# The first loads of an attention and experts kernel: half a weight slice first, six units on GpSimd's queue, scores ahead for one unit only

## The chip, the cores and the metric

The kernel runs on one core of a Trainium2 chip. The metric is the device time of one execution in microseconds (us), lower is better: the median of three runs is 1036.33 us. The engines are called by what they do: TensorE multiplies matrices, VectorE and ScalarE work on elements, GpSimd is used for some element work and issues transfers, and SyncE only issues transfers. In the profile they stand as PE (with its weight loads as PEld), DVE, ACT, POOL and SP.

## What is computed

Three parts run one behind the other, cut here to what matters:

```python
# 1: decaying linear attention; 4 batches, 8 heads, 768 steps, 64 wide
gamma = 1.0 - 2.0 ** (-5.0 - np.arange(H))
for t in range(S):
    state = gamma[None, :, None, None] * state + einsum('bhd,bhe->bhde', k[:, :, t], v[:, :, t])
    y[:, :, t] = scale * einsum('bhd,bhde->bhe', q[:, :, t], state)
# 2: x is y as (3072, 512); two weights of 512 x 2048 and 2048 x 512
h = x @ w_in
x = where(h > 0, h, exp(minimum(h, 0)) - 1) @ w_out
# 3: experts; 8 of them, each takes its 384 best of the 3072 tokens
logits = x @ w_gate
out[mask_e] = maximum(x[mask_e] @ w1[e], 0) @ w2[e]
```

## The kernel before

**Attention.** The 768 steps are cut into 6 chunks of 128. A unit is one chunk of one batch, all 8 heads of it, so there are 24 units, numbered from 0 here; two units make a block of 256 tokens, and there are 12 blocks. Units 0 to 3 are the first chunks of the four batches. For a unit, `load_units` (L349) brings q and k in transposed form into the tile `qk` and k and v in plain form into `kv`, 512 KB each; both tags have two buffers, so unit k takes the buffers of unit k - 2. `scores` (L393) multiplies k by q into `sc`, `masks` (L409) multiplies by the decay mask into `A` (in the first chunks by `hmask`, later by a triangle out of `csb`, with q decayed beforehand), `attend` (L419) multiplies v by `A` into `py`, together with the state `st` in later chunks. `y_out` (L438) splits `py` into a rounded part `yH` on ScalarE and a rest `yL` on VectorE. `carry` (L451) makes the new state from k and the decayed v through `pu`, and counts the unit as done. `decays` (L370) multiplies v by its decay on VectorE, in place; in the first chunks that waits until `attend` has read v. The thread `attention` (L474) goes through the units in that order. Its flag `ahead` puts the scores of unit k + 1 before the attend of unit k, for k below 3 where that unit's loads are issued already.

**Weights of part 2.** `w_in` and `w_out` arrive as 64-bit floats, each in 8 slices of two halves. A half is a tile `rw` of 512 KB. `load_weights` (L499) issues them on SyncE's queue in the order of the list `slices`: w1 slice 0, w1 slice 1, w2 slice 0, w1 slice 2, w2 slice 1 and so on. Every half is narrowed by hand: `scales` (L526) scales the high words on ScalarE or VectorE, `narrow` (L540) makes one shift (TENSOR_SCALAR) and two merges (SCALAR_TENSOR_TENSOR) into `n_rw` on VectorE, `highs` (L571) rounds to `w1H` or `w2H` on ScalarE, `lows` (L583) subtracts into `w1L` or `w2L` on VectorE. Slice 0 is narrowed half by half, the others by pairs. 

**Products.** For block n and slice i, `first_product` (L598) needs `yH` and `yL` of both units of the block and slice i of w1; its 24 matmuls fill one of two banks `ph`. `elus` (L634) makes `e`, `gH` and `gL` of it on ScalarE and VectorE, with two buffers of each. `second_product` (L664) needs these and slice i of w2, 12 matmuls into `px`. `seconds` (L687) runs the second products in the order in which the first ones were issued. Blocks 0 and 1 are worked on together, slice by slice, as the weights come.

**Who sets the order.** Nothing is ordered at run time: each engine and each queue runs a fixed list in order, and waits where an operand is not there. The lists come from a scheduler that runs at build time. Every activity above is a thread with a rank (lower goes first), `Sched.run` always advances the thread whose next instruction can start first by the model in `Plan` (L95), and `Plan.note` (L162) books durations, buffers and transfers. Transfers are one queue in that model, with 310 bytes per ns, and 150 for a plain load of GpSimd. In the kernel before, `load_units` (rank 0) and `load_weights` (rank 1) share SyncE's queue. It issues, at the start: the two halves of unit 0's `qk` (256 KB each), `hmask` (512 KB), unit 0's `kv`, `csb` (326 KB), `rcs` (4.5 KB), unit 1's `qk` and `kv`, and then the weights, with the later units' loads in between.

The lines that issue these loads are short:

```python
yield on("SP", ap.slot("kv"), when=lambda: did["unit"] > k - 2)
...
ahead = k < 3 and did["unit_load"] > k + 1
if ahead:
    yield from scores(k + 1)
yield from attend(k)
```

Parts 1 and 2 overlap until about 650 us; then come the routing of the tokens and the experts, whose code is not touched. The accumulating transfers that GpSimd issues in part 3 (`w1L<-e1R`) have the size of a unit's `qk`, 512 KB.

Of the kernel before, what the change touches and what calls it, by code (L numbers as in the profile page):

```python
# [44 lines left out]
BUSY = 8  # L45
# [49 lines left out]
class Plan:  # L95
# [66 lines left out]
    def note(self, eng, op, out, ins):  # L162
        o = out.tensor.name
        start = max([self.free[eng]] + [self.ready.get(x.tensor.name, 0.0) + self.gap(x.tensor.name, eng) for x in ins])
        if eng != "PE" or self.writer.get(o) != "PE":
            start = max(start, self.used.get(o, 0.0) + 140)
        if eng == "PE":
            end = start + self.pe_cost(op, ins, start)
            if start > self.free[eng] + 20:
                end += 100  # L170
        else:
            end = start + self.cost(eng, op, out, ins)
        self.free[eng] = end
        self.writer[o] = eng
        if "dma" in op:
            nb = self.size(out if out.space != "DRAM" else ins[0]) * P * 4
            self.dma = max(self.dma, end + 600) + nb / (150.0 if op == "dma_start" and eng == "POOL" else 310.0)
            end = self.dma + 1300
        for x in ins:
            k = x.tensor.name  # L180
            self.used[k] = max(self.used.get(k, 0.0), end)
        self.used[o] = max(self.used.get(o, 0.0), end)
        self.ready[o] = max(self.ready.get(o, 0.0), end) if "dma" in op or eng == "PE" else end
# [107 lines left out]
def on(eng, *needs, when=None, rank=None):  # L291
    return eng, needs, when, rank
# [3 lines left out]
def body(ctx: ExitStack, tc, qkv, w_in, w_out, w_gate_t, w1, w2, hm, cst, rc, rmat, out, dbg=None):  # L296
# [3 lines left out]
    PE, ACT, DVE, POOL, SP = (  # L300
        Engine(e, n, plan)
        for e, n in ((nc.tensor, "PE"), (nc.scalar, "ACT"), (nc.vector, "DVE"), (nc.gpsimd, "POOL"), (nc.sync, "SP"))
    )
    engines = {"ACT": ACT, "DVE": DVE, "POOL": POOL}
    ctx.enter_context(tc.manual_schedule())
    sched = Sched(plan)
    did = Counter()
# [7 lines left out]
    rcs = cp.tile([P, 1 + E], F32, name="rcs")  # L315
# [17 lines left out]
    ap = Tiles(s1.enter_context(tc.tile_pool(name="ap", bufs=2)), plan, 2)  # L333
    csb = c1.tile([P, cst.shape[1]], F32, name="csb")
# [13 lines left out]

    def load_units():  # L349
        for k, (b, c) in enumerate(seq):  # L350
            yield on("SP", ap.slot("kv"), when=lambda: did["unit"] > k - 2)
            qk, kv = (ap.tile([P, 2, H * D], F32, tag=tag, name=f"{tag}{k}") for tag in ("qk", "kv"))
            for part in ([0], [1]) if k == 0 else ([0, 1],):
                SP.dma_start(qk[:, part[0] : part[-1] + 1], qkv[b, c][:, part[0] : part[-1] + 1])
            if k == 0:
                SP.dma_start(hmask, hm)
            SP.dma_start(kv, qkv[b, c][:, 2:])
            if k == 0:
                SP.dma_start(csb, cst)
                SP.dma_start(rcs, rc)  # L360
            units[k] = {
                "qT": qk[:, 0].rearrange("p (a b) -> p a b", a=NP),
                "kT": qk[:, 1].rearrange("p (a b) -> p a b", a=NP),
                "k": kv[:, 0].rearrange("p (h d) -> p h d", h=H),
                "v": kv[:, 1].rearrange("p (h d) -> p h d", h=H),
                "q0": qk[:, 0],
            }
            did["unit_load"] += 1
# [24 lines left out]
    def scores(k):  # L393
        if k < 4:
            spare["tags"] = ("at", "at", "am", "m")
        elif k < 2 * tail + 2 and did["xcopy"] > 1:
            spare["tags"] = ("at", "at", "am")
        else:
            spare["tags"] = ("at", "at")
        yield on("PE", bank_slot(spare_tag()), *([csb] if seq[k][1] else []), when=lambda: did["decay_q" if seq[k][1] else "unit_load"] > k)  # L400
        u = units[k]
        u["sc"] = [spare_bank(f"sc{k}_{hh}") for hh in range(2)]
        for pr in range(NP):
            for hh in range(2):
                yield on("PE", u["q0"])
                sl = slice(hh * D, hh * D + D)
                PE.matmul(u["sc"][hh][:, pr * P : (pr + 1) * P], u["kT"][sl, pr, :], u["qT"][sl, pr, :], start=True, stop=True)

    def masks(k):  # L409
        u = units[k]  # L410
        u["A"] = []
        for hh in range(2):
            mask = tri if seq[k][1] else hmask[:, hh * NP * P : (hh + 1) * NP * P].rearrange("p (a b) -> p a b", a=NP)
            yield on("DVE", u["sc"][hh], ap.slot(f"A{hh}", 1), mask)
            a = ap.tile([P, NP, P], F32, tag=f"A{hh}", bufs=1, name=f"A{k}_{hh}")
            DVE.tensor_tensor(a, u["sc"][hh].rearrange("p (a b) -> p a b", a=NP), mask, op=OP.mult)
            u["A"].append(a)

    def attend(k):  # L419
        b, c = seq[k]  # L420
        yield on("PE", bank_slot(spare_tag()), when=lambda: c == 0 or did["decay"] > k)
        u = units[k]
        u["py"] = py = spare_bank(f"py{k}")
        heads = [(pr, hh, slice(hh * D, hh * D + D)) for pr in range(NP) for hh in range(2)]
        if c > 0:
            for pr, hh, sl in heads:
                yield on("PE", st)
                PE.matmul(py[sl, pr * P : (pr + 1) * P], st[sl, b, pr, :], u["qT"][sl, pr, :], start=pr == 0, stop=False)
        for pr, hh, sl in heads:
            yield on("PE", u["A"][hh], u["v"])  # L430
            PE.matmul(py[sl, pr * P : (pr + 1) * P], u["v"][:, 2 * pr + hh, :], u["A"][hh][:, pr, :], start=c == 0 and pr == 0, stop=pr == NP - 1)

        did["attended"] += 1
# [4 lines left out]
    def y_out(k):  # L438
        n, i = k // 2, k % 2
        py = units[k]["py"]  # L440
        yield on("ACT", py, ap.slot("yH"), when=lambda: y_free(n))
        if i == 0:
            ytiles[n] = [ap.tile([P, NP, BLK], F32R, tag=f"y{x}", name=f"y{x}{n}") for x in "HL"]
        yh, yl = (y[:, :, i * P : (i + 1) * P] for y in ytiles[n])
        pv = py.rearrange("p (a b) -> p a b", a=NP)
        copy("ACT", yh, pv)
        yield on("DVE", yh, ap.slot("yL"))
        DVE.tensor_sub(yl, pv, yh.bitcast(F32))
        did["y"] += 1
# [24 lines left out]
    def attention():  # L474
        ahead = False
        for k in range(len(seq)):
            if not ahead:
                yield from scores(k)
            yield from masks(k)
            ahead = k < 3 and did["unit_load"] > k + 1  # L480
            if ahead:
                yield from scores(k + 1)
            yield from attend(k)
            rest = [y_out(k), carry(k)]
            for part in rest if y_free(k // 2) else rest[::-1]:
                yield from part
            units.pop(k)
# [3 lines left out]
    hmask = stage[1].tile([P, 2 * NP * P], F32, tag="hm", bufs=1, name="hmask")  # L491
# [7 lines left out]
    def load_weights():  # L499
        m = 2 if wide else 1  # L500
        for s, (nm, i) in enumerate(slices):
            src = w_in if nm == "w1" else w_out
            x = src.bitcast(U32) if wide else src
            place = wp.slot(f"{nm}H{home[i]}") if i in home else stage[1].slot("raw", 2)
            before = 2 * NSTEP if (nm, i) == ("w2", NSTEP - 1) else 0
            yield on("SP", place, when=lambda: did["narrow"] > 2 * (s - 4) and did["low", nm] > 2 * (i - 4) and did["low", "w1"] >= before)
            for c in range(2):
                f = i * 256 + c * P
                if nm == "w1":
                    part = x[:, m * f : m * (f + P)].rearrange("(k p) (f w) -> p k f w", p=P, w=m)  # L510
                    shp = [P, KD, P, m]
                else:
                    part = x[f : f + P, :].rearrange("p (f w) -> p f w", w=m)
                    shp = [P, DM, m]
                if i in home:
                    tl = wp.tile(shp, x.dtype, tag=f"{nm}{'HL'[c]}{home[i]}", name=f"r{nm}{i}{c}")
                else:
                    tl = stage[1].tile(shp, x.dtype, tag="raw", bufs=2, name=f"r{nm}{i}{c}")
                SP.dma_start(tl, part)
                raws[(nm, i, c)] = tl  # L520
            did["weight"] += 1

    def words(r, w):
# [302 lines left out]
    quarter, part = rmb[:, o + 72 : o + 76], {4: rmb[:, o + 76 : o + 80], 2: rmb[:, o + 80 : o + 82]}  # L826
# [509 lines left out]
```

## Time and profile before

| what | value |
| --- | --- |
| median of 3 runs | 1036.33 us (1035.9 to 1037.97) |
| the profiled execution | 1035.3 us |
| its span, from the first to the last instruction | 1033.5 us |
| mean granted clock of TensorE | 0.985 |
| busy in the span: TensorE, VectorE | 975.4 us (94%), 730.2 us (71%) |
| busy in the span: ScalarE, GpSimd | 389.8 us (38%), 151.0 us (15%) |
| SyncE's queue, GpSimd's queue | 85.04 MB, 29.37 MB |

The times of the rows below are those of the profiled execution, counted from the start of its span. Busy tenths are given for 40 equal slices of the span, 9 meaning 90% or more. In a timeline a row is one instruction or several of a kind; behind its names and shapes stands in brackets how long the engine had been idle before it, and what ended that wait. All compute instructions are recorded at L208, a helper's line, so groups are told apart by the names of their tiles.

### The profile page before, as it was taken

Reading aid. Unit: us, or ns where it says so; the run is one execution under the profiler, and the core shown is the slowest. Engines: PE = TensorE matmul, PEld = TensorE weight load, DVE = VectorE, ACT = ScalarE, POOL = GpSimd, SP = SyncE. Lnnn points to the kernel's source line nnn. Section 1 sums busy time; section 2 is a strip of 40 time slices with the busy share of each in tenths; the row PEclk is TensorE's granted clock in tenths of the full one; section 3 lists DMA queues with packets and bytes.
Section 4 is the critical chain, followed back from the end, with each engine's and each line's share of the span. In section 5 each row is a group of like instructions: output and inputs, shape, how many; then the busy total and the mean of one; then the engine's idle time right before and its main releaser. Section 6 shows DMA issues by size and latency. Waiting matters only on the chain.

```text
span 1033.5 us, 17471 instructions
## 1 busy us (share of the span) xinstructions
PE 975.4 (94%) x6899; PEld 839.4 (81%) x6899; DVE 730.2 (71%) x1843; ACT 389.8 (38%) x603; POOL 151.0 (15%) x164
## 2 busy tenths in 40 slices
PE   2889999999999999999999999987999999999996
PEld 2778887888888888888888899765787888888895
DVE  4989979899989899664746364567777778777320
ACT  3555522223232232323333335123445345444441
POOL 0000012120211112010210000002213122134121
PEclk9999999999999999999999999996999999999998
DMA  9871243030303021111110000036757677678832
GB/s 330 294 244 62 84 141 102 1 103 1 103 1 103 1 65 38 62 42 53 51 61 2 10 13 1 12 105 191 209 139 233 183 192 224 177 194 236 252 93 62
DMA packets 56114, 115.52 MB, mean 112 GB/s; under 512 B 4192, under 2 KB 28768, under 8 KB 55904
## 3 DMA queue, kind: packets, MB, share of 16 engines
q1 hardware_dynamic: 47584, 85.04, 24.8%
q0 software_dynamic: 8448, 29.37, 11.8%
q8 instruction: 54, 0.88, 0.3%
q14 instruction: 28, 0.23, 0.1%
HBM read 85.03 MB, written 12.58 MB: 94 GB/s over the span
## 4 chain that ended last, share of the span: by engine, by line
PE 74%; DVE 11%; issue 7%; DMA 3%; ACT 2%; POOL 1%; POOLq 0%; SPq 0%; DVEq 0%; ACTq 0%
PE px L208 23%; PE ph L208 22%; PE po L208 10%; PE eh L208 10%; DVE junk L208 5%; PE py L208 3%; PE sc L208 2%; DMA xg<-xd,idx 2%; DVE junkw L208 2%; DVE gL L208 1%; PE pt L208 1%; DVE e L208 1%; PE pu L208 1%; PE lacc L208 1%; PE pc L208 1%
## 5 line engine op out<-in xcount | busy, mean ns | idle before, releaser
L208 PE MATMUL ph<-yH,w1H 128*128 128x256 f32 x768 | 220.3, 287 | 12.4 <-DVE e L208 10.2
L208 PE MATMUL ph<-yL,w1H 128*128 128x256 f32 x768 | 216.4, 282 | 0.1
L208 PE MATMUL ph<-yH,w1L 128*128 128x256 f32 x768 | 216.2, 281 | 0.0
L208 PEld LDWEIGHTS ph<-yH,w1H 128*128 128x128 f32 x768 | 146.0, 190 | 18.3 <-DVE e L208 12.1
L208 PEld LDWEIGHTS ph<-yH,w1L 128*128 128x128 f32 x768 | 146.0, 190 | 1.2
L208 PEld LDWEIGHTS ph<-yL,w1H 128*128 128x128 f32 x768 | 146.0, 190 | 0.4 <-DVE yL L208 0.3
L208 PE MATMUL px<-w2H,gH 128*128 128x512 f32 x332 | 134.2, 404 | 0.0
L208 DVE SCALAR_TENSOR_TENSOR junk<-x,wgb 128x512 f32<-128x512 f32 x160 | 128.1, 801 | 5.1 <-ACT x L208 1.2
L208 PE MATMUL px<-w2H,gL 128*128 128x512 f32 x332 | 131.2, 395 | 0.4 <-DVE gL L208 0.4
L208 PE MATMUL px<-w2L,gH 128*128 128x512 f32 x332 | 131.1, 395 | 0.0
L208 ACT ACTIVATE e<-ph 128x512 f32<-128x512 f32 x96 | 57.1, 594 | 186.9 <-PE ph L208 185.5
L208 DVE SCALAR_TENSOR_TENSOR e<-e,ph 128x512 f32<-128x512 f32 x96 | 65.6, 684 | 56.8 <-ACT e L208 56.7
L208 DVE SCALAR_TENSOR_TENSOR junkw<-wsum,wgb 128x512 f32<-128x512 f32 x128 | 89.2, 697 | 15.1 <-POOL wsum L208 12.7
L208 ACT ACTIVATE gH<-e 128x512 fp32r<-128x512 f32 x83 | 52.4, 632 | 103.0 <-DVE e L208 76.2
L208 PE MATMUL eh<-xTH,w1H 128*128 128x384 f32 x256 | 89.1, 348 | 0.3 <-ACT xTH L208 0.3
L208 PE MATMUL eh<-xTH,w1L 128*128 128x384 f32 x256 | 88.5, 346 | 0.3 <-DVE w1L L208 0.3
L208 PE MATMUL eh<-xTL,w1H 128*128 128x384 f32 x256 | 88.7, 347 | 0.0
L208 ACT ACTIVATE hH<-eh 128x384 fp32r<-128x384 f32 x64 | 31.4, 491 | 136.3 <-PE eh L208 130.9
L208 DVE TENSOR_TENSOR gL<-e,gH 128x512 fp32r<-128x512 f32 x83 | 64.4, 776 | 22.4 <-ACT gH L208 21.1
L208 PE MATMUL po<-w2H,hH 128*128 128x512 f32 x192 | 78.3, 408 | 0.0
L208 PE MATMUL po<-w2L,hH 128*128 128x512 f32 x192 | 77.5, 403 | 0.0
L208 PE MATMUL po<-w2H,hL 128*128 128x512 f32 x192 | 77.4, 403 | 0.0
(166 smaller groups left out, 1709.0 us busy)
## 6 DMA issues: line engine op xcount, KB each, us to landing
e1R<-in_w_dram SPq DMA_DIRECT2D x32, 512.0 KB, 6.0
e2R<-in_w_dram SPq DMA_DIRECT2D x32, 512.0 KB, 4.8
kv<-in_qkv_dram SPq DMA_DIRECT2D x24, 512.0 KB, 5.0
qk<-in_qkv_dram SPq DMA_DIRECT2D x23, 512.0 KB, 4.3
rw<-in_moe_w_in_dram SPq DMA_DIRECT2D x16, 512.0 KB, 9.5
rw<-in_moe_w_out_dram SPq DMA_DIRECT2D x16, 512.0 KB, 9.0
w1L<-e1R POOLq DMA_DIRECT2D x16, 512.0 KB, 7.2
w2L<-e2R POOLq DMA_DIRECT2D x16, 512.0 KB, 6.6
```

The source lines that it names most:

```text
L208: r = real(*args, **kw)
```

## The change

`load_units` now waits until one weight half has been issued, and `load_weights` pauses three times in its first two slices, so that the first issues of SyncE's queue are: first half of w1 slice 0, both halves of unit 0's `qk`, second half of w1 slice 0, `hmask`, unit 0's `kv`, unit 1's `qk` and `kv`, `csb`, `rcs`, and then w1 slice 1 and what follows. Units 2 to 7 are issued by GpSimd, the later ones by SyncE as before. Scores of the next unit come ahead of a unit's attend for unit 0 alone. The model's rate for a load of GpSimd out of the chip's main memory is now 310; transfers within the chip keep 150.

```diff
@@ Plan.note @@
-            self.dma = max(self.dma, end + 600) + nb / (150.0 if op == "dma_start" and eng == "POOL" else 310.0)
+            self.dma = max(self.dma, end + 600) + nb / (150.0 if out.space != "DRAM" and ins[0].space != "DRAM" else 310.0)
@@ load_units @@
-            yield on("SP", ap.slot("kv"), when=lambda: did["unit"] > k - 2)
+            q = "POOL" if 1 < k < BUSY else "SP"
+            dma = engines.get(q, SP).dma_start
+            yield on(q, ap.slot("kv"), when=lambda: did["unit"] > k - 2 and did["halves"] > 0)
             qk, kv = (ap.tile([P, 2, H * D], F32, tag=tag, name=f"{tag}{k}") for tag in ("qk", "kv"))
-            for part in ([0], [1]) if k == 0 else ([0, 1],):
-                SP.dma_start(qk[:, part[0] : part[-1] + 1], qkv[b, c][:, part[0] : part[-1] + 1])
             if k == 0:
-                SP.dma_start(hmask, hm)
-            SP.dma_start(kv, qkv[b, c][:, 2:])
-            if k == 0:
-                SP.dma_start(csb, cst)
-                SP.dma_start(rcs, rc)
+                for i in range(2):
+                    dma(qk[:, i : i + 1], qkv[b, c][:, i : i + 1])
+                did["qk"] += 1
+                yield on("SP", when=lambda: did["halves"] > 1)
+                dma(hmask, hm)
+            else:
+                dma(qk, qkv[b, c][:, :2])
+            dma(kv, qkv[b, c][:, 2:])
+            if k == 1:
+                dma(csb, cst)
+                dma(rcs, rc)
@@ attention @@
-            ahead = k < 3 and did["unit_load"] > k + 1
+            ahead = k == 0 and did["unit_load"] > k + 1
@@ load_weights @@
             for c in range(2):
+                if s < 2:
+                    yield on("SP", when=lambda: did["unit_load"] > 1 if s else c == 0 or did["qk"])
...
                 raws[(nm, i, c)] = tl
+                did["halves"] += 1
```

## Rows read from the trace of the kernel before

**Rows 1.** The page, busy tenths of TensorE and VectorE in 40 slices.
```profile
PE   2889999999999999999999999987999999999996
DVE  4989979899989899664746364567777778777320
```

**Rows 2.** Stretches: from:to, length, busy us (instructions) of PE, PEld, DVE, ACT, POOL; PEclk.
```profile
0.00:15.50 15.50, 6.04 (x48) 5.17 (x48) 1.29 (x2) 1.95 (x2) 0.20 (x4) 1.00 0.85 292
15.50:34.40 18.90, 7.14 (x69) 5.86 (x67) 18.46 (x35) 11.31 (x19) 0.00 (x0) 1.00 1.04 384
34.40:74.00 39.60, 35.58 (x311) 31.41 (x312) 34.67 (x63) 20.76 (x36) 0.00 (x0) 0.96 0.70 233
74.00:100.00 26.00, 26.00 (x151) 22.67 (x151) 25.69 (x48) 15.13 (x26) 0.00 (x0) 1.00 0.30 115
100.00:150.00 50.00, 50.00 (x401) 43.90 (x401) 40.42 (x78) 22.45 (x39) 2.69 (x2) 1.00 0.33 117
```

**Rows 3.** Timeline of TensorE up to 30 us: start, us, what, idle before it.
```profile
5.99 2.08 PE L208 MATMUL sc<-qk 64*128 64x128 f32 x16 [5.99 <-DMA qk<-in_qkv_dram]
11.54 2.08 PE L208 MATMUL sc<-qk 64*128 64x128 f32 x16 [3.48 <-DMA qk<-in_qkv_dram]
13.55 1.97 PE L208 MATMUL py<-A,kv 128*64 128x128 f32 x16
...
25.65 2.17 PE L208 MATMUL sc<-qk 64*128 64x128 f32 x16 [8.21 <-DMA qk<-in_qkv_dram]
27.75 1.97 PE L208 MATMUL py<-A,kv 128*64 128x128 f32 x16
```

**Rows 4.** Timeline of VectorE: masks, decays of v, yL, and low parts at 75.85.
```profile
17.82 1.28 DVE L208 TENSOR_TENSOR A<-sc,hmask 128x512 f32<-128x512 f32 x2
...
32.46 0.68 DVE L208 TENSOR_TENSOR kv<-kv,csb 128x512 f32<-128x512 f32 x1
...
33.66 0.68 DVE L208 TENSOR_TENSOR yL<-py,yH 128x512 fp32r<-128x512 f32 x1
...
72.46 0.69 DVE L208 TENSOR_TENSOR kv<-kv,csb 128x512 f32<-128x512 f32 x1 [1.49 <-DMA kv<-in_qkv_dram]
...
75.85 1.29 DVE L208 TENSOR_TENSOR w2L<-n_rw,w2H 128x512 fp32r<-128x512 f32 x2
```

**Rows 5.** The chain that ended last, in order of time: start, us, what.
```profile
34.39 4.27 PE ph L208 x22
...
73.81 3.10 PE ph L208 x24
...
79.96 16.57 PE px L208 x71
```

**Rows 6.** Timeline of ScalarE: the first and the third weight half scaled.
```profile
14.32 0.67 ACT L208 ACTIVATE rw<-rw 128x512 f32<-128x512 f32 x1 [12.29 <-DMA rw<-in_moe_w_in_dram]
...
17.32 0.66 ACT L208 ACTIVATE rw<-rw 128x512 f32<-128x512 f32 x1 [0.57 <-DMA rw<-in_moe_w_in_dram]
```

**Rows 7.** VectorE's groups by form up to 100 us: busy us, mean ns of one.
```profile
L208 DVE SCALAR_TENSOR_TENSOR n_rw<-rw,n_rw 128x512 uint32<-128x512 uint32 x50 | 32.2, 683 | 0.1
...
L208 DVE TENSOR_SCALAR n_rw<-rw 128x512 uint32<-128x512 uint32 x26 | 10.1, 419 | 0.0
...
L208 DVE TENSOR_TENSOR w1L<-n_rw,w1H 128x512 fp32r<-128x512 f32 x12 | 7.8, 683 | 0.0
```

**Rows 8.** Tile w1L, 690 to 900 us: GpSimd's issues (min/median/max ns), and their landing.
```profile
L208 POOL DMA_DIRECT2D w1L<-e1R x10: 845/1000/1031, 702.2 to 880.1; - x10
...
DMA to landing us min/median/max: 4.5/4.7/8.6
```

**Rows 9.** TensorE's waits in the whole span: us in total, times, longest.
```profile
PE ph L208 <- DVE e L208: 10.2, 8, 2.5
```

## The prediction

> **What bounds the kernel now.** I read the page first, and in it the two rows of tenths [rows 1]: TensorE stands at 8 or 9 in nearly every one of the 40 slices of 25.8 us, and at 2 in the first. VectorE stands at 4 in that slice and then at 8 to 9 for the next dozen. So the kernel is bound by TensorE's work, its loss at the head is the largest single one, and behind the head a second engine is nearly as full. The table by stretches says how much [rows 2]: up to 34.4 us TensorE is busy 6.04 + 7.14 = 13.2 us, so 21.2 us are lost; in the 39.6 us up to 74 it loses 4.0 us; from 74 to 150 us it loses nothing. VectorE is idle for 14.2 of the first 15.5 us, then loses 0.4 us, 4.9 us and 0.3 us up to 100 us. What is won in the head reaches the end if TensorE, from 74 us on, finds its work as early as it can use it.
>
> The timeline of the head says why TensorE is idle. The scores of unit 0 start at 5.99 us, when its q and k have landed; those of unit 1 wait until 11.54 us for theirs; those of unit 2 wait 8.21 us until 25.65 us, and in TensorE's fixed order the product py of unit 1 stands behind them, at 27.75 us [rows 3]. The masked scores that py of unit 1 reads were done at 17.82 + 1.28 = 19.10 us [rows 4]. So 8.6 us of that wait are order alone. Behind it, VectorE decays v of unit 1 at 32.46 us and writes its yL by 33.66 + 0.68 = 34.34 us, and the first products run without a break from 34.39 us [rows 4, 5].
>
> **When a transfer lands.** The queue is in order and its bytes are known, so four landings give a line: unit 0's q and k end after 512 KB and are used at 5.99 us; unit 1's q and k after 4.64 times that (hmask, k and v, the 326 KB of constants, itself) at 11.54 us; the first weight half after 6.64 at 14.32 us; the third after 8.64 at 17.32 us [rows 3, 6]. From the first to the last that is 11.33 us for 7.64 loads, 1.48 us each: a load that ends after u of them is usable at 4.5 + 1.48u.
>
> **Half a weight slice leads.** The new order on SyncE's queue is weight half 0 (u = 1), q and k of unit 0 (2), weight half 1 (3), hmask (4), k and v of unit 0 (5), q and k of unit 1 (6), its k and v (7), constants (7.64), then weights as before. By the line: first half 6.0 us instead of 14.3; unit 0's scores 7.5 instead of 6.0; second half 8.9; hmask 10.4, behind scores that end near 9.6; q and k of unit 1 at 13.4 instead of 11.5. The constants (15.8) are first read by the decay of v of unit 0, later than that, so they cost nothing; without that cover the decay would wait for them.
> The gain is VectorE's work that falls into its idle head. A half costs one shift (419 ns), two merges (683 each) and one low part (683): 2.47 us, so slice 0 costs 4.94 us [rows 7], and all of it fits ahead of the decay of v of unit 0.
> The cost is that decay itself: it waits for py of unit 0, which stands behind unit 1's scores. Those come 1.9 us later by the line.
>
> **Units two to seven (counted from 0) on GpSimd's queue.** Twelve loads of 512 KB leave SyncE's queue. Each issue costs GpSimd about 1.0 us [rows 8], 12 us in all, on an engine with nothing else to do in this stretch; if it had work for px then, the issue that waits for a free buffer would hold it back. SyncE's queue loses these waits: no weight load stands behind a buffer of kv any more. The price of that cover is seen once: VectorE waits 1.49 us for a kv at 72.46 us [rows 4]. I don't count it as won, since another wait can take its place.
> In return q and k of unit 2 no longer queue behind the weights: unit 0's buffer is free when its scores end, at 9.6 us, so this load meets those of unit 1. No row here has two queues in the head. It delays unit 1 by nothing at one end (the line has no second queue in it, so it can't gain) and by a whole load, 1.48 us, at the other; I take half, 0.75 us, since it starts with half of them landed. The Trainium skill, "DMA: Bandwidth & Descriptors", section on SWDGE, HWDGE and iDMA, says that each DMA engine serves its queues in turn; by it the full 1.48 us would be nearer, and the sum below 0.7 us smaller. No run so far shows it.
> So py of unit 0 ends 1.9 + 0.75 = 2.6 us later, near 18.2 us. VectorE's lead from there on is 4.94 - 2.6 = 2.3 us (1.6 to 3.1 between the ends).
>
> **Scores ahead only for unit 1.** Py of unit 1 follows its masked scores at 19.10 + 2.6 = 21.7 us instead of 27.75: 6.0 us earlier. From its end (27.75 + 1.97) to the end of yL VectorE took 4.6 us, and needs only 0.69 + 0.68 of it. So the steady first products start between 25.2 and 28.3 us instead of 34.39: **TensorE's lead is 6 to 9 us.** Unit 2's scores fall behind these products; at best they run where TensorE was idle anyway.
>
> **The sum.** Two leads differ, 2.3 us on VectorE and 6 to 9 us on TensorE, so I ask which arrives. The place to read it is 72 to 80 us. Second products run in a fixed order, and the third of them needs slice 2 of the second weight, whose low parts are written at 75.85 + 1.29 = 77.14 us [rows 4]. First products can't run far ahead, as there are two banks and two buffers of each kind. TensorE runs one at 73.81 us and one behind it, and from 79.96 us a block of 71 matmuls of second products, six products at one go [rows 5]. So the block started 2.8 us after its weights. If all of TensorE's work came 6 to 9 us earlier, the weights would decide: they come 2.3 us earlier, and the block can start 2.3 + 2.8 = **5.1 us earlier**. From there TensorE is full up to 150 us, so this is the gain at the end. Its bounds: 1.6 + 2.8 = 4.4 us with the whole shared load, 5.1 + 1.5 = 6.6 us if the wait for kv goes too, 9 us if VectorE never decides. The profiled execution took 1035.3 us with a span of 1033.5, and the median is 1036.33; 1.0 us is inside the spread. From the profiled one the sum gives 1030.2 us, on the median's scale **1031.2 us**.
>
> **Rivals.**
> *TensorE's lead arrives whole.* The list scheduler may put products of the second block before slice 2, so that second products need fewer weights; then 7 to 9 us arrive, 1027.3 to 1029.3 us. For it: VectorE's 4.9 idle us from 34.4 to 74 us [rows 2]. Against: it is full on both sides.
> *Given back.* Four loads (units 2 and 3) now overtake weights; 4 x 1.48 = 5.9 us of delay for the weights is more than VectorE's lead, and VectorE then starves for 5 us between 25 and 60 us. Or it costs later: the plan's rate for loads on GpSimd's queue is changed for these twelve alone, and takes no time itself, but the plan writes the whole order anew. VectorE's e holds up a first product 8 times for 10.2 us, 2.5 us at the longest [rows 9], and two more such waits cancel the gain. Then 1034.3 to 1038.4 us.
> *Slower: GpSimd's transfers land late.* TensorE's order is fixed by a plan that believes a queue of 310 bytes per ns. If the kv of units 2 to 7 lands later than planned, py waits in order, as the scores did for 8.21 us [rows 3]; that wait in place of the 5.1 us won gives 1036.33 + 8.21 - 5.1 = 1039.4 us. It decides once a load takes some 10 us from issue to landing, as unit 2's kv can be issued near 20 us and is wanted near 30. GpSimd's transfers of this size, accumulating ones within the chip's memory, take 4.5 to 8.6 us later on, and an issue at most 1031 ns [rows 8], which speaks against it. The Trainium skill, "SBUF — State Buffer", section "SBUF: two separate sides", has the rule for it: VectorE in its two-port mode locks GpSimd out of writing descriptors. VectorE's shifts, at 419 ns against 683 for other operations of this size [rows 7], look like that mode; but one of them is over in 0.4 us, and the rows of GpSimd's issues beside a busy VectorE show no such stretch.
> That the change doesn't do what it says I leave out as a case: each of its edits moves an issue or drops a branch.
>
> **How the numbers follow.** VectorE's pace (3 to 7 us won, 1029.3 to 1033.3 us) 0.50; TensorE's lead whole 0.15; given back 0.20; slower 0.15. 0.2% is 2.1 us, about what a measurement can tell from no change. The first two are faster by more: 0.65; same 0.20; slower 0.15. The range reaches from the whole lead to the far end of "given back", 1027 to 1038 us, and leaves out some 0.15, mostly above.
>
> **What would show it.** VectorE's first shift stands near 7 us; scores of unit 0 at 7.5 and of unit 1 near 14; py of unit 1 at 21 to 23 us with no scores ahead of it; steady first products by 28 us; no wait of SyncE's queue for kv below 70 us; the long block of second products near 75 us. It is wrong if TensorE waits for a transfer of GpSimd's queue, if VectorE waits for weights between 20 and 60 us, or if the lead at 80 us is there and gone at 700.

## The result and the profile after

The changed kernel takes **1024.26 us** (median of four runs, 1022.24 to 1024.35) against 1036.12 us in the same comparison: 0.988 of it, with a 95% interval of 0.986 to 0.990. It is 11.9 us faster, where 5.1 us were forecast and 1027 us was the lower end of the range. The sign was right, the size was not.

The span of the profiled execution is 1022.6 us instead of 1033.5, so 10.9 us less. First the head. The timeline of TensorE in the changed kernel, up to 34 us (start, us, what, idle before it), answers to [rows 3]:

```profile
7.24 2.08 PE L208 MATMUL sc<-qk 64*128 64x128 f32 x16 [7.24 <-DMA qk<-in_qkv_dram]
12.92 2.08 PE L208 MATMUL sc<-qk 64*128 64x128 f32 x16 [3.60 <-DMA qk<-in_qkv_dram]
14.92 1.97 PE L208 MATMUL py<-A,kv 128*64 128x128 f32 x16
17.69 1.12 PE L208 MATMUL pu<-kv 128*64 128x64 f32 x16 [0.79 <-DVE kv L208]
19.98 2.52 PE L208 MATMUL py<-A,kv 128*64 128x128 f32 x16 [1.17 <-issue]
...
24.95 0.58 PE L208 MATMUL ph<-yL,w1H 128*128 128x256 f32 x1
...
33.81 0.58 PE L208 MATMUL ph<-yH,w1L 128*128 128x256 f32 x1 [3.99 <-DVE w1L L208]
```

Unit 1's py starts at 19.98 us instead of 27.75, with no scores ahead of it, and the steady first products at 24.95 us instead of 34.39. At 33.81 us they have waited 3.99 us for VectorE's low parts of the next slice. VectorE's timeline of the changed kernel answers to [rows 4]:

```profile
5.13 0.43 DVE L208 TENSOR_SCALAR n_rw<-rw 128x512 uint32<-128x512 uint32 x1 [5.13 <-ACT rw L208]
...
22.54 0.69 DVE L208 TENSOR_TENSOR kv<-kv,csb 128x512 f32<-128x512 f32 x1 [0.79 <-PE py L208]
23.16 0.69 DVE L208 TENSOR_TENSOR yL<-py,yH 128x512 fp32r<-128x512 f32 x1
...
71.65 1.28 DVE L208 TENSOR_TENSOR w2L<-n_rw,w2H 128x512 fp32r<-128x512 f32 x2
```

The first weight half is shifted at 5.13 us; the decay of unit 1's v and its yL follow py at once; the low parts of slice 2 of the second weight are done at 72.93 us instead of 77.14. The stretches of the changed kernel, with the columns of [rows 2], give the head as a sum:

```profile
0.00:15.50 15.50, 4.66 (x38) 4.17 (x40) 6.11 (x10) 3.85 (x5) 1.00 (x5) 1.00 0.84 302
15.50:34.40 18.90, 12.26 (x89) 10.27 (x86) 13.36 (x25) 10.16 (x17) 1.62 (x3) 0.93 1.06 386
34.40:74.00 39.60, 37.01 (x347) 33.56 (x347) 38.70 (x71) 22.81 (x39) 3.17 (x6) 0.95 0.83 304
74.00:100.00 26.00, 26.00 (x141) 22.18 (x140) 25.56 (x47) 17.00 (x29) 0.00 (x0) 1.00 0.00 1
100.00:150.00 50.00, 50.00 (x427) 44.06 (x427) 40.99 (x81) 21.49 (x37) 3.80 (x4) 1.00 0.34 116
```

Up to 74 us TensorE is busy 53.9 us instead of 48.8, so 5.2 us more, and from there to 150 us it is full in both kernels. Busy time is work only where the clock is the same. The table has 1.00 for the first stretch, but the profile has no record of the clock there, and TensorE's rows show that it stood at the lower level, 1.2 GHz: the first products start 0.21 us apart up to 28.1 us in the changed kernel and up to 37.5 us before, as they do again in the stretch recorded at 0.50 below (34.20, 34.41, 34.62 us), and 0.12 us apart from then on. In the changed kernel:

```profile
27.68 0.41 PE L208 MATMUL ph<-yL,w1H 128*128 128x256 f32 x1
27.89 0.41 PE L208 MATMUL ph<-yH,w1H 128*128 128x256 f32 x1
...
28.39 0.28 PE L208 MATMUL ph<-yH,w1H 128*128 128x256 f32 x1
28.50 0.28 PE L208 MATMUL ph<-yH,w1L 128*128 128x256 f32 x1
```

and before:

```profile
36.91 0.41 PE L208 MATMUL ph<-yH,w1L 128*128 128x256 f32 x1
37.12 0.41 PE L208 MATMUL ph<-yL,w1H 128*128 128x256 f32 x1
...
37.66 0.28 PE L208 MATMUL ph<-yL,w1H 128*128 128x256 f32 x1
37.78 0.28 PE L208 MATMUL ph<-yH,w1H 128*128 128x256 f32 x1
```

After that the changed kernel fell to 0.50 once more, in and behind the wait that ends at 33.81 us, and the kernel before to 0.57 from 54 to 58 us, behind waits of 1.17 and 0.69 us. The first of these lines is the changed kernel's, the second the kernel before's (the number behind POOL's is the share of full speed that was granted):

```profile
31.70:38.30 6.60, 4.49 (x21) 4.49 (x22) 6.51 (x13) 3.81 (x8) 0.00 (x0) 0.50 1.05 387
```

```profile
54.00:58.00 4.00, 3.61 (x27) 3.27 (x28) 3.50 (x8) 1.97 (x4) 0.00 (x0) 0.57 0.45 159
```

The three nearly cancel: with the busy time at the lower level counted half, TensorE has done some 44.3 us of work instead of 38.9, 5.4 us more, an estimate from the busy times and these moments.

How the gain grows behind that is read off the chain of waits, piece against piece. These pieces are the changed kernel's:

```profile
63.03 11.50 PE ph L208 x96
74.53 8.40 PE px L208 x36
...
649.08 5.68 PE px L208 x24
...
676.78 3.44 PE px L208 x15
```

and these two are the kernel before's, behind its block at 79.96 us in [rows 5]:

```profile
657.18 5.67 PE px L208 x24
...
684.98 3.43 PE px L208 x15
```

The long block comes 5.4 us earlier, the pieces near 650 and 680 us 8.1 and 8.2 us, and the end 10.9 us. So about half of the gain stands behind the block, which is itself another one than before (36 matmuls at one go instead of 71). The kernel before's piece of 24 has no fixed place: two kernels of the second and third set, `before_late` and `before_x`, run its lists without any change up to about 700 us, and have this piece at 655.29 and 655.14 us. Measured from these, the gain near 650 us is 6.1 to 6.2 us and not 8.1. Part of the middle is TensorE's clock. The table by stretches for 177 to 181 us of the kernel before, and for 175 to 179 us of the changed kernel (the columns of [rows 2]):

```profile
177.00:181.00 4.00, 3.38 (x16) 3.38 (x17) 3.94 (x11) 2.38 (x4) 0.00 (x0) 0.57 0.00 0
```

```profile
175.00:179.00 4.00, 4.00 (x20) 3.25 (x19) 3.94 (x11) 2.13 (x4) 0.00 (x0) 1.00 0.00 0
```

Before, this stretch ran mostly at 1.2 GHz; after, at 2.4. In both kernels TensorE had just waited for VectorE's e, 2.52 us up to 177.62 us before and 2.29 us up to 172.14 us after. At 0.57 the busy 3.38 us cost some 1.5 us against full speed, an estimate from this line, of the 2.7 us by which the gain grows between the block and 650 us.

### The profile page after: what moved, and what is told of

Its sections match the earlier page's. It is cut to its first block, busy times and chain, and to the rows that moved or that the text cites. A ratio compares the mean times of both kernels' runs of the same rounds, so it can differ in the third digit from the quotient of the medians.

```text
span 1022.6 us, 17495 instructions
## 1 busy us (share of the span) xinstructions
PE 973.6 (95%) x6899; PEld 838.3 (82%) x6899; DVE 731.1 (72%) x1843; ACT 389.5 (38%) x603; POOL 160.7 (16%) x176
## 4 chain that ended last, share of the span: by engine, by line
PE 77%; DVE 13%; issue 6%; DMA 3%; ACT 1%; POOL 0%; SPq 0%; POOLq 0%; DVEq 0%
PE px L208 22%; PE ph L208 22%; PE eh L208 12%; PE po L208 11%; DVE junk L208 7%; PE py L208 3%; PE sc L208 2%; DMA xg<-xd,idx 2%; PE pt L208 1%; DVE e L208 1%; DVE n_rw L208 1%; PE pu L208 1%; DMA qk<-in_qkv_dram 1%; DVE gL L208 1%; DVE A L208 1%
## 5 line engine op out<-in xcount | busy, mean ns | idle before, releaser
L208 DVE TENSOR_TENSOR gL<-e,gH 128x512 fp32r<-128x512 f32 x83 | 62.1, 749 | 21.3 <-ACT gH L208 19.5
## 6 DMA issues: line engine op xcount, KB each, us to landing
rw<-in_moe_w_in_dram SPq DMA_DIRECT2D x16, 512.0 KB, 11.9
```

The lines of the kernel that those rows point to most:

```text
L208: r = real(*args, **kw)
```

## The experiments

Twelve kernels were run beside the kernel before, each in five rounds; 0.1% is 1.0 us. Two words of the expectations need telling. The **lead** at a moment is how much earlier TensorE has done the same work than in the profile of the kernel before: its matmuls are summed up in order of time, each with its usual distance from start to start. And the **late order** is TensorE's list of instructions from the routing on, near 650 us.

### First set: the parts alone

The scores edit alone (`ahead_only`):

```diff
-            ahead = k < 3 and did["unit_load"] > k + 1
+            ahead = k == 0 and did["unit_load"] > k + 1
```

> The kernel before with the one edit on the scores (ahead for unit 0 alone). Theory A (the lead that TensorE holds from 80 to 150 us is VectorE's lead plus the 2.8 us of slack before the long block of second products): VectorE wins nothing here, so the lead is 0 to 2.8 us, though first products start some 6 us earlier than 34.39 us. Rival (TensorE's own start decides): the lead is 6 us. In either case what the changed kernel gained behind 150 us (5.8 us of its 10.9) stays if it belongs to any lead (whole time 1028 to 1030), and goes if it was a matter of one order (1033 to 1036).

Measured: 1029.4 us, 0.9933 (0.9907 to 0.9959). In its profile the first products run from 24.3 us on, and the lead is 4.4 us at 100 us and 5.4 us at 640 us. That is between the two theories for the head, and well above theory A's 2.8 us. The time lies in the range given for a gain behind 150 us that belongs to any lead; the second set shows that this doesn't follow, since this kernel also has the changed kernel's late order.

Half a weight slice first, alone, with every unit on SyncE's queue (`lead_only`: the changed kernel with `q = "SP"` and `ahead = k < 3`):

> The kernel before with only the new order of first issues (half a weight slice first), all on SyncE's queue, scores ahead as before. Theory A: py of unit 1 still stands behind unit 2's scores and their transfer, so first products start near 34 us; VectorE is 3.5 us ahead, TensorE gains 0 to 1 us, time 1034 to 1037. Rival (VectorE's earlier work alone makes the gain): lead at 150 us 3.5 us or more, time 1032 or less.

Measured: 1044.74 us, 1.0102 (1.0070 to 1.0133). Neither theory had it slower. The profile is of its fastest run, 1042.25 us.

Units 2 to 7 on GpSimd's queue, alone (`pool_only`; cut: its loads go through `dma`, and the plan's rate is the changed kernel's):

```diff
-            yield on("SP", ap.slot("kv"), when=lambda: did["unit"] > k - 2)
+            q = "POOL" if 1 < k < BUSY else "SP"
+            dma = engines.get(q, SP).dma_start
+            yield on(q, ap.slot("kv"), when=lambda: did["unit"] > k - 2)
```

> The kernel before with only units 2 to 7 on GpSimd's queue, first issues and scores ahead as before. Theory A: unit 2's q and k land before 20 us, its scores wait little, py of unit 1 comes some 7 us earlier even with the scores ahead of it; VectorE wins only the waits behind SyncE's queue, 0 to 2 us; lead at 150 us 2.8 to 5 us, time 1028 to 1033. Rival (the edit on the scores is what frees py): lead under 1 us, time 1035 to 1037.

Measured: 1035.3 us, 0.9994 (0.9971 to 1.0017): nothing. The rival held, and the trace says why. TensorE's timeline of this kernel:

```profile
18.67 0.46 PE L208 MATMUL sc<-qk 64*128 64x128 f32 x2 [1.43 <-issue]
19.32 2.04 PE L208 MATMUL sc<-qk 64*128 64x128 f32 x14 [0.19 <-DVE A L208]
21.29 1.71 PE L208 MATMUL py<-A,kv 128*64 128x128 f32 x16
31.48 0.58 PE L208 MATMUL ph<-yH,w1H 128*128 128x256 f32 x1 [8.48 <-ACT yH L208]
```

and ScalarE's and VectorE's of the same kernel:

```profile
27.09 0.68 ACT L208 ACTIVATE rw<-rw 128x512 f32<-128x512 f32 x1 [2.85 <-DMA rw<-in_moe_w_in_dram]
...
30.84 0.58 ACT L208 ACTIVATE yH<-py 128x512 fp32r<-128x512 f32 x1
```

```profile
32.53 0.68 DVE L208 TENSOR_TENSOR kv<-kv,csb 128x512 f32<-128x512 f32 x1
```

Unit 2's data came early, as theory A said, and py of unit 1 was done at 23.0 us instead of 29.7. But yH waits until 30.84 us and the decay of v until 32.53 us, almost where they stood before, with no idle time in front of them: both engines work off weights first. ScalarE even stood idle for 2.85 us up to 27.09 us, waiting for a weight, while py was there. Their lists were written by a plan that counts on unit 2's transfer behind all weights issued so far. The wait is in the lists, not in the transfer.

The changed kernel without the scores edit (`no_ahead`, `ahead = k < 3` again):

> The changed kernel with the scores ahead for units 1 to 3 as before. Theory A: unit 2's transfer is early on its own queue, so scores ahead cost nothing and the time is that of the changed kernel, 1023 to 1025. Rival (order of scores matters by itself): py of unit 1 waits again, 3 us or more of the gain go, 1027 or more.

Measured: 1037.67 us, 1.0015 (0.9997 to 1.0033). All of the gain goes (some of it with the late order, see the table below), and in the head by the same mechanism: py of unit 1 at 22.37 us, and then, in TensorE's timeline of this kernel,

```profile
33.70 0.58 PE L208 MATMUL ph<-yH,w1H 128*128 128x256 f32 x1 [9.35 <-ACT yH L208]
```

### Second set: one part left out, and the late order alone

> The changed kernel with every unit's loads on SyncE's queue again (half slice first, scores ahead for unit 0 alone). Theory B (the edit on the scores frees py and yL of unit 1 in the fixed lists, and carries most of the gain; a weight half first pays only where weights don't wait behind a kv buffer on SyncE's queue): first products start near 25 us as in the changed kernel, weights then wait behind kv, some of the lead is lost by 80 us: time 1026 to 1031. Rival (GpSimd's queue only saves issue time): as the changed kernel, 1023 to 1025.

`no_pool` has `q = "SP"` for all units. Measured: 1024.53 us, 0.9889 (0.9863 to 0.9916). The rival held: GpSimd's queue gives nothing that shows here either. The lists of TensorE, VectorE and ScalarE are the changed kernel's from the first instruction to the last.

> The changed kernel with the first loads in the old order (units 2 to 7 on GpSimd's queue, scores ahead for unit 0 alone). Theory B: first products start some 2 to 3 us after those of the scores edit alone, held by w1L of slice 0 as there, and from 40 us on no weight waits behind a kv: 1025 to 1030, between the scores edit alone (1029.4) and the changed kernel. Rival (the half slice first is what the rest needs): no better than the scores edit alone, 1029 or more.

`no_lead` is `pool_only` with the scores edit. Measured: 1032.4 us, 0.9961 (0.9944 to 0.9978), slower than the scores edit alone, as the rival said. That doesn't decide for the rival, as the two have different late orders (below).

For the other two, a shift goes into the plan's model of TensorE's clock when the routing is planned. It changes no instruction and no list up to there:

```diff
+        self.off = 0.0
...
-        tick = int(start // self.TICK)
+        tick = int((start + self.off) // self.TICK)
...
     did["late"] = 1
+    plan.off = 1800.0
```

> The changed kernel with the plan's clock model shifted by 1.8 us from the routing on: the same instructions and the same order up to some 650 us, another order behind. Theory C (the gain behind 650 us, 2.9 us of span, is one draw among orders): the time moves by 1 us or more, either way, and the lead at 640 us stays 7.8 us to within 1. Rival (the later gain belongs to the earlier start): within 1 us of the changed kernel.

Measured: 1027.54 us, 0.9912 (0.9890 to 0.9933), 3.3 us slower than the changed kernel, with a lead of 7.6 us at 640 us against its 7.8.

> The kernel before with the same shift of the plan's clock model from the routing on, and nothing else. Theory C: 1 us or more from the kernel before, either way. Rival: within 1 us of it. A gain of some 3 us here would say that the changed kernel's gain behind 650 us could be had without any of its edits.

Measured: 1032.19 us, 0.9976 (0.9956 to 0.9995), 3.5 us faster than the kernel before. **Theory C held in both.** The lists of all kernels behind the routing, by names without their buffer numbers, fall into a few late orders: one for the changed kernel, `no_pool` and `ahead_only`; one for the kernel before, `pool_only` and `no_lead`; one for both shifted kernels and `no_ahead`; one for `lead_only`. Within a group TensorE's lists are equal to the instruction, but for up to 10 of the 2110 matmuls behind the first of the routing, which stand elsewhere in `pool_only`, `no_lead` and `no_ahead`. So each of the parts had drawn a late order too, and the first set had mixed two things.

### Third set: heads and late orders crossed

A shift of -0.1 us gives the kernel before the changed kernel's late order, and one of 0.3 us gives the changed kernel that of the kernel before. In these pairs, and between the two shifted kernels and `lead_z` below, the lists of all five engines are the same from 430 us on; and a shift leaves all lists of a kernel as they were up to 706 us (652 us for the shift of 3.0 us).

> The kernel before with the plan's clock model shifted by -0.1 us from the routing on. The lists up to some 650 us are those of the kernel before; behind it TensorE's list is the changed kernel's, to the instruction. Theory D (the change's gain is its head's, 4.7 us as between the two shifted kernels, plus a draw of the late order worth 6 to 7 us): 1029 us, some 6 to 7 us faster than the kernel before with none of the change's edits. Rival (the late order is worth the 3 us that the two profiles show): 1032 to 1033.

Measured: 1031.71 us, 0.9962 (0.9943 to 0.9980). Faster by 4 us with none of the edits; that is between theory D's 6 to 7 and the rival's 3. Its profile has a span of 1030.1 us, 3.4 us less than the kernel before's. Of these, 2.0 us stand ahead of the routing, where the lists are the same (the piece of 24 at 655.14 us instead of 657.18), and only 1.3 us behind it.

> The changed kernel with a shift of 0.3 us from the routing on, which gives it the late list of the kernel before. Theory D: the head's gain alone is left, 1030 to 1031.5 us. Rival (the whole gain belongs to the edits): 1024 to 1026.

Measured: 1029.21 us, 0.9935 (0.9910 to 0.9960). The rival falls; theory D was 0.8 us short on the head.

> Half a slice first alone, with a shift that gives it the late order of the two shifted kernels of the second set (1032.2 without the edit, 1027.5 with the whole change). Theory D: the 9 us that this edit lost were mostly its late order; by its lead at 640 us (-0.2 us against 1.8) it now takes 1033 to 1036. Rival (the edit alone hurts the head that much): 1040 or more.

Measured: 1038.17 us, 1.0022 (1.0003 to 1.0042). Some 7 to 8 of the 10 us that this edit had lost were its late order; against the kernel before with the same late order (0.9976) it still loses 4.8 us, more than theory D had. VectorE's timeline of this kernel shows the first place (L209, as the shift adds a line to the code):

```profile
35.75 0.68 DVE L209 TENSOR_TENSOR kv<-kv,csb 128x512 f32<-128x512 f32 x1
36.35 0.68 DVE L209 TENSOR_TENSOR yL<-py,yH 128x512 fp32r<-128x512 f32 x1
```

Those stood at 32.46 and 33.66 us [rows 4]. The weights are there earlier, the plan puts their conversions first, and unit 1's values come later. How the rest of the 4.8 us comes about was not shown: `lead_only`, with the same lists up to the routing, has the piece of 24 at 657.19 us, as the kernel before has, and `lead_z` at 662.11.

> The changed kernel with a shift of 3.0 us from the routing on: a late order that no kernel so far has had. Theory D: anything from 1021 to 1036, as orders drawn so far differ by up to 7 us and more; it is a draw for a faster version. Rival: 1024 to 1026 like the changed kernel.

Measured: 1032.37 us, 0.9965 (0.9950 to 0.9980): a late order that costs 8 us against the changed kernel's. No kernel run here beats the changed one; `no_pool` equals it, and their profiles differ by 0.1 us in span.

Ratios to the kernel before, by head and late order (`lead_only` with 1.0102 and `after_v` with 0.9965 have late orders of their own):

| head | late order of the changed kernel | of the kernel before | of the shifted kernels |
| --- | --- | --- | --- |
| before | 0.9962 | 1 | 0.9976 |
| scores edit | 0.9933 | | |
| GpSimd's queue | | 0.9994 | |
| half slice first | | | 1.0022 |
| half slice and scores | 0.9889 | | |
| GpSimd's queue and scores | | 0.9961 | |
| half slice and GpSimd's queue | | | 1.0015 |
| all three | 0.988 | 0.9935 | 0.9912 |

Down a column stands the head: all three edits give 0.82%, 0.65% and 0.64%, **6.6 to 8.5 us**. Along a row stands the late order: 0.38% and 0.55% from the kernel before's to the changed one's, **3.9 to 5.7 us**. Either way round the two make up the 12 us. By the intervals above each of these differences is uncertain by 2 to 3 us, but none reaches zero.

The edits by themselves are seen where two rows share a column. The scores edit is worth 3.0 us alone (0.9962 to 0.9933, not clear of noise), 3.4 us beside GpSimd's queue (0.9994 to 0.9961), and **10.7 us** beside both others (1.0015 to 0.9912). The half slice costs 4.8 us without the scores edit (0.9976 to 1.0022), and gives 4.6 us (0.9933 to 0.9889) or 2.7 us (0.9961 to 0.9935, not clear of noise) with it. GpSimd's queue moves nothing by more than 0.1%.

Where the late order costs is seen in part between the changed kernel and `after_y`, whose piece of 24 second products stands at 649.51 us, 0.4 us behind the changed kernel's, and whose span is 1027.7 us, 5.1 us longer. TensorE's waits from 640 us on, and the stretch from 720 to 760 us, in `after_y`:

```profile
PE pt L209 <- DMA xg<-xd,idx: 6.2, 5, 2.5
```

```profile
720.00:760.00 40.00, 37.23 (x229) 29.62 (x227) 26.93 (x96) 19.58 (x26) 10.66 (x13) 0.96 0.73 198
```

and in the changed kernel:

```profile
PE pt L208 <- DMA xg<-xd,idx: 3.2, 3, 1.4
```

```profile
720.00:760.00 40.00, 38.10 (x242) 30.80 (x242) 29.71 (x109) 18.81 (x25) 12.06 (x14) 1.00 0.77 211
```

With the other order the transposes wait 3.0 us longer for gathered tokens, and the granted clock is 0.96 instead of 1.00 over 40 us, 1.6 us of full speed. That is 4.6 of the 4.7 us that are added behind 650 us; that the two simply add was not shown. The other pair with these two late orders bears out the first only. The kernel before, with the list of `after_y`, and `before_x`, with the changed kernel's:

```profile
PE pt L208 <- DMA xg<-xd,idx: 4.8, 5, 1.8
```

```profile
PE pt L209 <- DMA xg<-xd,idx: 3.4, 4, 1.7
```

The wait is 1.4 us longer, about the 1.3 us that are added behind the routing, and the clock is 1.00 from 720 to 760 us in both. So the wait for gathered tokens goes with the order in both pairs; the lower clock doesn't. That the runs have 3.9 us where this pair of profiles has 1.3 us behind the routing stays open.

## Why the prediction was right and wrong

**Landings.** The line held in its slope and was late at its start: unit 0's scores 7.24 us (7.5 forecast), unit 1's 12.92 (13.4, or 14.1 with half a shared load); only the very first half came 1.6 us earlier than by the line, at 4.44 us on ScalarE. The shared load cost nothing that shows: unit 1's scores stand at 12.92 us with GpSimd's queue and at 12.67 us in `no_pool`, and three more profiles of the changed lists have them at 12.65 to 12.95 us. The Trainium skill's rule of queues served in turn ("DMA: Bandwidth & Descriptors", section on SWDGE, HWDGE and iDMA) pointed to the upper end of 1.48 us; these profiles lie at the lower.

**TensorE's lead in the head.** Forecast 6 to 9 us; first products came 9.4 us earlier, a little above. VectorE took v and yL of unit 1 at once. (The early end of the forecast adds up to 25.0 us, not 25.2: 21.7 + 1.97 + 0.69 + 0.68.)

**VectorE's lead, and the block.** Forecast 2.3 us and 5.1 us; the weights of the block came 4.2 us earlier and the block 5.4 us. That the block agrees so well is luck: the sum's 2.3 + 2.8 us were 4.2 + 1.2. VectorE does cut TensorE's lead, but not there: of the 9.4 us, 3.99 us go in the wait at 33.81 us for the low parts of w1's next slice, in which the clock falls as well. From 53.6 to 82 us TensorE has no wait at all. The block stands 1.6 us behind its weights instead of 2.8, held by TensorE's own first products (96 matmuls from 63.03 us on). The same lists profiled as `before_x` have the block at 77.74 us instead of 79.96, so the 5.4 us are uncertain by 2. The head's gain over the runs, 6.6 to 8.5 us, lies above the term's 5.1 and inside its bounds of 4.4 to 9.

**Half a slice first, by itself.** Here a reason failed. I gave this part VectorE's 4.94 us of earlier work as a gain of its own. Alone it costs 4.8 us; with the scores edit it is worth 4.6 us (0.9889 against 0.9933), or 2.7 us in the other late order. And dropping the scores ahead, which I took for a gain of its own too, carries most of the head only together with it: 3.0 us alone, 10.7 us beside the half slice and GpSimd's queue. Work put earlier on one engine is a gain only where the lists put it in front of nothing that is wanted sooner.

**Units on GpSimd's queue.** I listed the waits that it takes off SyncE's queue, and counted them as nothing. That held: 0.06%, and no difference with the other two edits in place. An issue took 0.53 to 0.80 us, not 1.0, beside a VectorE that was busy for 52.1 of the 58.5 us from 15.5 to 74 us. The rival of late transfers did not happen: up to 640 us TensorE waited for no transfer but those of unit 0's and unit 1's q and k, which are SyncE's. The lock that the Trainium skill tells of ("SBUF — State Buffer", section "SBUF: two separate sides") left no mark in these issues.

**The step that failed.** "From there TensorE is full up to 150 us, so this is the gain at the end." The sum had no term for what comes behind. I knew that "the plan writes the whole order anew", but put that down under the costs, as two more waits of 2.5 us at most, and took the kernel before's late order for neutral. It is one draw among several that lie up to 8 us apart (1024.26 to 1032.37 us with the changed head), and the change moved the kernel from a slower one to the fastest drawn here: 3.9 to 5.7 us by the runs. That is luck; nothing in the edits aims at it. With that term, open to both sides, the range would have reached below 1024 us. The term for the head was small as well, 5.1 us against 6.6 to 8.5.

**What was to show it.** VectorE's first shift near 7 us: 5.13. Py of unit 1 at 21 to 23: 19.98. Steady first products by 28: 24.95. No wait of SyncE's queue for kv: so. The long block near 75 us: 74.53. Of the signs of being wrong none came: TensorE waited for none of GpSimd's loads, and VectorE for no weight transfer between 20 and 60 us. And "the lead at 80 us is there and gone at 700": it was there and had grown.

## What to carry to other kernels

Where a scheduler at build time writes fixed lists, an edit's time is its own effect plus a new draw of every list behind it: shift the scheduler's clock in both kernels and compare them with the same late order before you credit the edit. A transfer that comes early frees nothing while the lists of the engines behind it still count on it late. And parts of such a change don't add: test them in pairs.

## What the runs showed of the hardware

TensorE's clock falls to its lower level, 1.2 GHz, in short stretches that are not the same in every execution of the same lists. The kernel before ran from 177 to 181 us at 0.57 of its speed. `before_x`, with the same lists up to the routing, did so too (0.57 from 176 to 180 us); `before_late`, with the same lists again, has no such stretch between 61 and 695 us. What the engine did before was alike: it had waited for e for 2.52, 2.50 and 2.40 us. In the changed kernel it had waited for 2.29 us and the clock stayed at 1.00; in `after_y`, the same lists, it had waited for 1.87 us and the clock fell.

Landings differ as well: unit 1's q and k let its scores start at 11.54, 10.54 and 11.28 us in the three profiles of the kernel before's lists. These three reach the piece of 24 near 655 us at 657.18, 655.14 and 655.29 us. So two profiles of one kernel differ by about 2 us there without any edit, and the 8.1 us read at 650 us hold some of that. `before_x` is 2 us earlier in spite of its slow stretch, so the clock is not the whole of it.
